# Stand-in matmuls at the start, and two VectorE pieces of step 12 placed sooner, in a spectral filter with a SiLU feed-forward block on one core

## The chip, the cores and the metric

One core of a Trainium2 chip runs the whole program. The metric is the device time in microseconds (us) of one execution; smaller is better. TensorE is called PE here, its weight loads PEld; VectorE is DVE, ScalarE is ACT, GpSimd is POOL, SyncE is SP.

## The reference

Eight sequences of 3008 tokens with 256 channels go through a global spectral filter, and the result of all tokens through a feed-forward block with SiLU:

```python
def _attn_ref(x, filt_r, filt_i) -> np.ndarray:
    X = np.fft.rfft(x, axis=1)
    F = (filt_r + 1j * filt_i)[None, :, :]
    Y = X * F
    y = np.fft.irfft(Y, n=x.shape[1], axis=1)
    return y.astype(np.float32)
...
def _moe_ref(x, w_in, w_out) -> np.ndarray:
    h = x @ w_in
    g = h * (1.0 / (1.0 + np.exp(-h)))
    return (g @ w_out).astype(np.float32)
```

w_in is 256 x 2048, w_out 2048 x 256, all in 32-bit floats.

## The kernel before, in words

**The filter.** Each batch's Fourier transform is split into short transforms (3008 = 47 x 64) that are matmuls with tables. Its stages have PSUM tiles by which the profile names them: pa (first stage, lines 401 and 425), pb (second stage, L542), a product with the filter on DVE (`multiply`, L635, which writes z and p) and two sums of products (`add`, L643 and L644), pc (the way back, L656 and L676), a store to DRAM and a load in another order, and pd (the last stage, L742), which is copied to y (L761).

**The feed-forward block.** Tokens are handled in 48 pairs of tiles of up to 256 columns each, and each pair in 8 steps, one for 256 of the 2048 hidden channels. The two 2 x 2 products of a step are formed with seven matmuls each in place of eight, from sums and differences. The operands' differences over tokens are made on DVE once per pair by `tokens(pair)`: three subtractions from y into a tile ty. `hidden(step)` makes the hidden values with matmuls into two PSUM banks, px and pyz (L1001), which ACT and DVE read: ACT copies partial sums to abc and takes SiLU (L1005), DVE adds (L972) to g. The half of pyz that a step calls zo is written by the matmul A12 and read by the first sum, g0; the half yo is written by S1 and S4 and read by the sums g2 and g1. `finish` makes the two last differences of g in the next step. `project(step)` multiplies g by w_out into four accumulator banks a0 to a3 (acc, L1093) one step later (LAG = 1), and `drain` copies a bank out, or adds it to what is there (s), when its pair has no matmul left on it. The first six steps are plain (`hidden_plain`, L1047), eight matmuls without the sums.

**What sets the order.** The schedule is written out by hand. The first batch's filter runs at the start, with nothing else for PE to do. From then on the loop goes over 384 steps of 8 rounds each. In a round the generators of `hidden` and `project` are advanced by one matmul each, and `until(time)` issues all pieces that are due in a list `pending`, sorted by time; `put(step, rnd, piece)` enters a piece. So the filter of the next batches is laid between the matmuls of the feed-forward block, piece by piece. A step in `opened` starts with the work of another stage, two projections of the step before ahead of it. Every engine runs its instructions in the order of issue.

The second batch (b = 1, at = 48) has a plan of its own in `plan`: for each of six groups g the pieces `forward`, `multiply` for two banks and `add` for two banks, with their steps and rounds counted from at. The forward of group 0 is issued when step 12 opens, so its listed place is not used. The pair 0 of tokens takes steps 0, 1 and 6 to 11, pair 1 steps 2 to 5 and 12 to 15, pair 2 steps 16 to 23. The accumulators of pair 0 are drained while step 12 runs.

**Banks at the start.** Until the loop starts, `bank` hands out the eight PSUM banks in turn by a counter `early[0]`: 2 banks f, then a0 to a3, then x and yz. The loop uses the banks by name.

**Stand-ins.** `idle(n, operand, m)` takes one bank and issues n matmuls of m columns by m columns whose result is never read:

```python
        ps = bank(0, "idle").rearrange("p a c -> p (a c)")
        rows = (wx_t if operand is None else operand)[:, 0:m]
        for _ in range(n):
            nc.tensor.matmul(out=ps[0:m, 0:m], lhsT=rows, rhs=rows, start=True, stop=True)
```

There are 26 of 36 columns ahead of pa, on a block of zeros, and 2 of 96 columns between the second batch's pa and the first batch's pd. Each matmul in 32-bit floats shows as two passes in the profile, a weight load and a matmul each.

Of the kernel before, what the change touches and what calls it, by code (L numbers as in the profile page):

```python
# [274 lines left out]
def kernel(  # L275
# [78 lines left out]
    def bank(b, name, spare=None):  # L354


        if early[0] is None and spare in ("x", "yz"):
            return xps.tile([128, 2, C], FP32, name=name, tag=spare)
        if early[0] is None and spare is not None:
            return accps.tile([128, 2, C], FP32, name=name, tag=f"a{spare}")  # L360
        if early[0] is None:
            return fps.tile([128, 2, C], FP32, name=name, tag="f")
        early[0] += 1
        k = early[0] % 8
        if k < 2:
            return fps.tile([128, 2, C], FP32, name=name, tag="f")
        if k > 5:
            return xps.tile([128, 2, C], FP32, name=name, tag="x" if k == 6 else "yz")
        return accps.tile([128, 2, C], FP32, name=name, tag=f"a{k - 2}")
# [451 lines left out]
    def put(step, rnd, piece, *args):  # L821

        pending.append((step + rnd / ROUNDS, len(pending), lambda: piece(*args)))
# [3 lines left out]
    def plan(b, part):  # L827

        at = STEPS * b

        if b > 1:
            put(at - {2: 80, 3: 120}.get(b, 128), 0, part["reverse_x"])
            early_fold = (-73, ((-68, 3), (-68, 5), (-65, 3), (-64, 3))), (-89, ((-82, 5), (-81, 3), (-81, 5), (-75, 5)))
            for f, step, load, places, ends in (
                    (0, -64, *early_fold[b > 2], ((1, 0), (1, 3))),
                    (1, -56, -63, ((-61, 5), (-60, 3), (-60, 5), (-59, 3)), ((1, 3), (2, 3))),
                    (2, -48, -55, ((-52, 3), (-52, 5), (-51, 5), (-50, 5)), ((1, 3), (2, 3)))):
                put(at + load, 4 if load == -89 else 0, part["load_fold"], f)
                for k, (fold_step, rnd) in enumerate(places):
                    put(at + fold_step, rnd, part["fold"], f, k)  # L840
                put(at + step, 7, part["stage1_fold"], f)
                put(at + step, 7, part["evict_fold"], f)
                for q, (after, rnd) in enumerate(ends):
                    put(at + step + after, rnd, part["pairs_fold"], f, q)
                joined.add(at + step)
                opened.add(at + step + 1)
            put(at - 47, 0, part["load_fold"], 3)
            for k, (step, rnd) in enumerate(((-45, 3), (-45, 5), (-44, 3), (-44, 5))):
                put(at + step, rnd, part["fold"], 3, k)
            early_out.add(at - 43)  # L850
            open_step(at - 43, (part["stage1_fold"], 3), (part["evict_fold"], 3))
            put(at - 43, 3, part["pairs_fold"], 3, 0)
            put(at - 43, 5, part["pairs_fold"], 3, 1)
            return plan_two(b, part)
        put(at - 38, 0, part["load_t2"], 0)
        put(at - 38, 0, part["load_t2"], 1)
        for g, places in enumerate((
                ((-36, 3), (-36, 5), (-35, 3), (-35, 5), (-34, 5)),
                ((-35, 6), (-34, 3), (-33, 3), (-33, 5), (-32, 1)),
                ((-32, 7), (-31, 0), (-31, 2), (-28, 5), (-27, 2)),  # L860
                ((-27, 3), (-27, 5), (-26, 5), (-25, 3), (-24, 3)),
                ((-24, 7), (-23, 0), (-23, 2), (-20, 2), (-20, 5)),
                ((-20, 3), (-19, 3), (-19, 5), (-18, 3), (-18, 5)))):
            pieces = (("forward", g), ("multiply", g, 0), ("multiply", g, 1), ("add", g, 0), ("add", g, 1))
            for (step, rnd), (piece, *args) in zip(places, pieces):
                if piece != "forward" or g in (1, 3, 5):
                    put(at + step, rnd, part[piece], *args)
        open_step(at - 36, *last_part[0](5), (part["forward"], 0))
        for g, step in ((0, -32), (2, -24), (4, -16)):
            put(at + step, 7, part["inverse"], g, 2)  # L870
            if g < 4:
                pending.append((at + step + 7 / ROUNDS, 10 ** 6 + 9, lambda g=g: part["forward"](g + 2, ACCS)))
                joined.add(at + step)
            put(at + step, 7, part["even"], g, 0, 2)
            put(at + step, 7, part["even"], g, 1, 2)
            put(at + step + 1, 5, part["rows"], g, 0, 2)
            put(at + step + 2, 3, part["rows"], g, 1, 2)
        plan_rest(b, part)
# [11 lines left out]
    def plan_two(b, part):  # L890

        at = STEPS * b
        put(at - 41, 3, part["load_t2"], 0)
        put(at - 41, 3, part["load_t2"], 1)
        for g, step, places in (
                (0, -40, ((-39, 3), (-38, 3), (-38, 5), (-36, 3), (-36, 5), (-35, 3))),
                (2, -32, ((-31, 0), (-31, 2), (-29, 5), (-28, 3), (-28, 5), (-27, 3))),
                (4, -24, ((-23, 0), (-23, 2), (-22, 3), (-21, 3), (-21, 5), (-19, 3)))):
            if g:
                plan_inverse(at + step, part, g - 2, *([((4, 3), (4, 5), (5, 5), (6, 3))] if g == 4 else []))  # L900
                opened.add(at + step + 1)
            put(at + step, 7, part["forward_two"], g)
            put(at + step, 7, part["free_two"], g)
            pieces = (("multiply_two", 0, 0), ("multiply_two", 0, 1), ("add_two", 0),
                      ("multiply_two", 1, 0), ("multiply_two", 1, 1), ("add_two", 1))
            for (place, rnd), (piece, *args) in zip(places, pieces):
                put(at + place, rnd, part[piece], g, *args)
        plan_inverse(at - 16, part, 4)
        plan_rest(b, part)

    def open_step(step, *pieces):

        opened.add(step)
        for piece, *args in pieces:
            pending.append((step - 0.06, len(pending), lambda piece=piece, args=args: piece(*args)))
# [62 lines left out]
    def tokens(pair):  # L978

        n, yt = pairs[pair][3], channels(pair)  # L980
        t = typool.tile([128, 4, CH], FP32, name=f"ty_{pair}", tag="ty")
        combine(v, t[:, 0:2, 0:n], yt[:, :, n:2 * n],
                yt[:, 0, 0:2 * n].rearrange("p (a n) -> p a n", a=2), ALU.subtract)
        combine(v, t[:, 2, 0:n], yt[:, 1, n:2 * n], t[:, 0, 0:n], ALU.subtract)
        combine(v, t[:, 3, 0:n], yt[:, 1, 0:n], t[:, 2, 0:n], ALU.subtract)
        ty[pair] = t
# [337 lines left out]
    def idle(n, operand=None, m=128):  # L1324
# [5 lines that stand above are left out]
# [8 lines left out]
    wide_rows = d_t[0:96].rearrange("p s r n -> p (s r n)")[:, 0:256]  # L1338
    blank = w_t.rearrange("p j c w n -> p (j c w n)")[0:96, 6144:6272]
    v.memset(blank, 0.0)  # L1340
    idle(26, operand=blank, m=36)

    part, second = spectral(0), spectral(1)
    part["load_first"]()
# [86 lines left out]
    def halves_of(*gs):  # L1431
        for g in gs:
            for i in range(2):
                part["store_half"](g, i, 1, gp)
    halves_of(2, 3)
    idle(2, m=96)
    early[0] -= 1
    part["stage3"](0)
    out_of(3, 3, copy=act)
# [23 lines left out]
    for b in range(1, B):  # L1463
        plan(b, second if b == 1 else spectral(b))
# [28 lines left out]
    per = len(PAIRS) * 2  # L1493


    combines = ((-2, 1), (6, 1), (11, 5), (22, 1), (26, 6), (38, 1))
    stores = (((10, 1), (10, 5)), ((19, 1), (23, 5)), ((31, 1), (31, 5)), ((35, 1), (35, 5)),
              ((43, 1), (43, 5)), ((50, 1), (51, 1)))
    for pair in range(len(pairs)):
        step, rnd = combines[pair % per] if pair > 2 else ((5, 2), (11, 1), (12, 1))[pair]  # L1500
        pending.append((pair // per * STEPS + step + rnd / ROUNDS, 98, lambda pair=pair: tokens(pair)))
        for chunk in range(2 if pair < len(pairs) - 1 else 0):
            step, rnd = stores[pair % per][chunk] if pair else (14, 1 + 4 * chunk)
            pending.append((pair // per * STEPS + step + rnd / ROUNDS, 99 + chunk,
                            lambda pair=pair, chunk=chunk: output(pair, chunk)))
# [65 lines left out]
```

## Time and profile before

| | |
|---|---|
| timed runs | 2484.73, 2486.55, 2486.83 us; median 2486.55 |
| profiled execution | 2485.27 us, its span 2483.1 us |
| busy in the span | PE 100%, PEld 86%, DVE 70%, ACT 44%, POOL 18% |
| PE by tile | acc 1513.1 us, px and pyz of L1001 1555 us (overlapping), all other lines 60 us or less |
| stand-ins | 52 passes of 36 columns, 4 passes of 96 columns |
| DMA | 69 GB/s mean over the span, 16 engines nearly full from 2 to 30 us |

Times in the profile count from the start of the span. A row of the timeline gives the start, the time taken, engine, line, operation, the tile written and those read, the shape, how many instructions were merged into it, and in brackets the idle time before it with what ended that. A row of waits reads: who waited, for whom, microseconds in total, how many times, the longest. Matmuls overlap in the pipe, so the duration of one says less than the distance from one start to the next.

### The profile page before, as it was taken

The numbers are of one execution on the slowest core, as the hardware profiler recorded it, in microseconds if no ns is written. First come the engines' busy times: TensorE is split into PE (matmuls) and PEld (weight loads), VectorE is DVE, ScalarE is ACT, GpSimd is POOL, SyncE is SP. The second block draws the span as 40 slices with busy tenths as digits, with TensorE's granted clock in tenths as the row PEclk, the third lists the DMA queues.
The fourth block names the chain that finished last, engine by engine and source line by source line (L and its number), as shares of the span: only waits on it lengthen the run. The fifth ranks groups of instructions, "written<-read, shape, count | busy, mean of one in ns | idle before, by whom it ended". The sixth has DMA issues, their size and how long they took to land.

```text
span 2483.1 us, 42315 instructions
## 1 busy us (share of the span) xinstructions
PE 2472.1 (100%) x16272; PEld 2124.9 (86%) x16272; DVE 1748.4 (70%) x3577; ACT 1087.1 (44%) x2986; POOL 438.9 (18%) x683
## 2 busy tenths in 40 slices
PE   9999999999999999999999999999999999999999
PEld 6888888888888888888888888889888888888988
DVE  7876777777777777786777767777777767655544
ACT  4534444444444444444444444444444444444443
POOL 4121112112221112211221112211221121101100
PEclk9999999999999999999999999999999999999999
DMA  8432225203242033320333114221142211200000
GB/s 327 148 98 77 74 63 117 63 14 93 61 109 61 25 78 81 96 54 26 88 83 89 49 29 108 60 69 43 51 98 47 56 51 32 59 22 9 17 10 17
DMA packets 139881, 170.68 MB, mean 69 GB/s; under 512 B 20972, under 2 KB 113484, under 8 KB 139148
## 3 DMA queue, kind: packets, MB, share of 16 engines
q1 hardware_dynamic: 116416, 121.74, 18.4%
q0 software_dynamic: 22272, 44.89, 6.9%
q8 instruction: 128, 2.10, 0.4%
q10 hardware_dynamic: 992, 1.36, 0.2%
q14 instruction: 73, 0.60, 0.1%
HBM read 96.06 MB, written 81.26 MB: 71 GB/s over the span
## 4 chain that ended last, share of the span: by engine, by line
PE 99%; DVE 0%; DMA 0%; POOL 0%; ACT 0%; issue 0%; SPq 0%; DVEq 0%
PE acc L1093 46%; PE px L1001 26%; PE pyz L1001 19%; PE pd L779 1%; PE pf L504 1%; PE pc L598 1%; PE pb L560 1%; PE pa L401 1%; PE pc L676 0%; PE px L1047 0%; PE pyz L1047 0%; PE pb L542 0%; PE pd L742 0%; PE pc L656 0%; DMA d<-w_t 0%; DMA w_t<-d 0%
## 5 line engine op out<-in xcount | busy, mean ns | idle before, releaser
L1093 PE MATMUL acc<-g,w_t 128*128 128x256 f32 (+1 forms) x5388 | 1513.1, 376 | 3.0 <-ACT o L792 2.5
L1093 PEld LDWEIGHTS acc<-g,w_t 128*128 128x128 f32 x5388 | 1019.8, 190 | 153.1 <-ACT o L792 15.3
L972 DVE TENSOR_TENSOR g<-pyz,abc 128x256 f32<-128x256 f32 (+1 forms) x1134 | 472.3, 416 | 468.2 <-ACT abc L1022 228.4
L972 DVE TENSOR_TENSOR g<-g 128x512 f32<-128x512 f32 (+1 forms) x1134 | 581.3, 513 | 193.8 <-ACT g L1005 180.8
L1001 PE MATMUL px<-ty,w_t 128*128 128x256 f32 (+1 forms) x2268 | 665.5, 375 | 0.0
L1005 ACT ACTIVATE g<-g 128x256 f32<-128x256 f32 (+1 forms) x1134 | 465.4, 410 | 231.9 <-DVE g L972 231.9
L972 POOL TENSOR_TENSOR s<-s 128x256 f32<-128x256 f32 (+1 forms) x331 | 254.3, 785 | 1436.4 <-DVE s L1121 981.8
L1001 PEld LDWEIGHTS px<-ty,w_t 128*128 128x128 f32 x2268 | 427.9, 190 | 52.1 <-issue 0.8
L1001 PE MATMUL pyz<-y,w_t 128*128 128x256 f32 (+1 forms) x1512 | 444.0, 375 | 1.1 <-DVE g L972 1.1
L1001 PEld LDWEIGHTS pyz<-y,w_t 128*128 128x128 f32 x1512 | 279.4, 189 | 42.3 <-DVE g L972 2.9
L1016 ACT COPY abc<-px 128x256 f32<-128x256 f32 (+1 forms) x378 | 139.1, 368 | 366.6 <-PE px L1001 366.6
L1005 ACT ACTIVATE g<-px 128x256 f32<-128x256 f32 (+1 forms) x378 | 143.5, 380 | 298.1 <-PE px L1001 298.0
L1022 ACT COPY abc<-px 128x256 f32<-128x256 f32 (+1 forms) x378 | 139.2, 368 | 307.3 <-PE px L1001 307.2
L1001 PE MATMUL px<-y,w_t 128*128 128x256 f32 (+1 forms) x756 | 223.5, 377 | 0.0
L1001 PE MATMUL pyz<-ty,w_t 128*128 128x256 f32 (+1 forms) x756 | 222.1, 376 | 0.0
L1001 PEld LDWEIGHTS px<-y,w_t 128*128 128x128 f32 x756 | 141.7, 189 | 21.1 <-DVE q L800 1.9
L1001 PEld LDWEIGHTS pyz<-ty,w_t 128*128 128x128 f32 x756 | 139.9, 190 | 20.2 <-DVE g L972 0.4
L1009 ACT COPY abc<-px 128x256 f32<-128x256 f32 (+1 forms) x378 | 133.0, 352 | 34.5 <-PE px L1001 34.5
L524 POOL DMA_DIRECT2D d<-tf x96 | 48.5, 505 | 212.9 <-DVE tf L454 212.9
L1121 ACT COPY s<-acc 128x512 f32<-128x512 f32 (+2 forms) x99 | 56.1, 566 | 49.0 <-issue 28.5
L619 POOL DMA_DIRECT2D d<-low x36 | 22.3, 618 | 292.5 <-DVE low L615 279.0
L494 DVE TENSOR_TENSOR uf<-x_all 120x512 f32<-120x512 f32 (+1 forms) x72 | 60.2, 864 | 0.3 <-issue 0.3
(134 smaller groups left out, 1390.2 us busy)
## 6 DMA issues: line engine op xcount, KB each, us to landing
t<-d SPq DMA_DIRECT2D x84, 256.0 KB
t<-d SPq DMA_DIRECT2D x224, 96.0 KB
out_dram<-s SPq DMA_DIRECT2D x64, 256.0 KB
d<-q POOLq DMA_DIRECT2D x48, 256.0 KB, 5.3
x_all<-in_x_dram SPq DMA_DIRECT2D x96, 96.0 KB
x_all<-xr SPq DMA_DIRECT2D x96, 96.0 KB
d<-tf POOLq DMA_DIRECT2D x96, 96.0 KB, 2.7
d<-tq POOLq DMA_DIRECT2D x96, 96.0 KB, 2.8
```

The source lines that it names most:

```text
L401: nc.tensor.matmul(out=ps[q], lhsT=wx3_t[rows, k], rhs=xs[j][rows, k], start=(k == 0), stop=(k == 2), skip_group_check=True)
L494: nc.vector.tensor_tensor(out=out, in0=in0, in1=in1, op=op)
L504: nc.tensor.matmul(out=ps[q][32 * k:32 * k + 32], lhsT=wq_t[rows, k], rhs=rhs[k][rows], start=True, stop=True)
L524: nc.gpsimd.dma_start(out=d1[par, :, grp, at:at + 4], in_=part[rows].rearrange("p q n c -> p (q n) c"))
L972: eng.tensor_tensor(out=out, in0=in0, in1=in1, op=op)
L1001: nc.tensor.matmul(out=out, lhsT=w_t[:, jp, c, 0], rhs=rhs, start=start, stop=True, skip_group_check=True)
L1005: nc.scalar.activation(out=g[:, k, 0:n], in_=g[:, k, 0:n] if src is None else src, func=AFT.Silu)
L1009: nc.scalar.copy(out=sums[:, 0, 0:n], in_=xo)
L1016: nc.scalar.copy(out=sums[:, 1, 0:n], in_=xo)
L1022: nc.scalar.copy(out=sums[:, 2, 0:n], in_=xo)
L1093: nc.tensor.matmul(out=acc[pair][i][:, h, 0:n], lhsT=w_t[:, jp, OUT_PLACE.get(c, c), 1], rhs=g[:, k, 0:n], start=i not in touched, stop=la ...
L1121: copy(out=dst, in_=src)
```

## The change

The stand-ins ahead of pa become 64 of 15 columns. The two between pa and pd go, and with them their step of the bank counter, so that stage pd of groups 0 to 2 takes other banks. The first filter product of the second batch, group 0 and bank 0, moves from step 12 round 5 to step 12 round 3. The tokens' sums of pair 2 move from step 12 round 1 to round 0.

```diff
         for g, places in enumerate((
-                ((-36, 3), (-36, 5), (-35, 3), (-35, 5), (-34, 5)),
+                ((-36, 3), (-36, 3), (-35, 3), (-35, 5), (-34, 5)),
                 ((-35, 6), (-34, 3), (-33, 3), (-33, 5), (-32, 1)),
...
     v.memset(blank, 0.0)
-    idle(26, operand=blank, m=36)
+    idle(64, operand=blank, m=15)
...
     halves_of(2, 3)
-    idle(2, m=96)
     early[0] -= 1
     part["stage3"](0)
     out_of(3, 3, copy=act)
...
     for pair in range(len(pairs)):
-        step, rnd = combines[pair % per] if pair > 2 else ((5, 2), (11, 1), (12, 1))[pair]
+        step, rnd = combines[pair % per] if pair > 2 else ((5, 2), (11, 1), (12, 0))[pair]
```

In DVE's order of instructions the three subtractions come to stand ahead of the sum g0 of step 12 instead of behind `finish`, and the two products ahead of the sum g2 of step 12 instead of between the drains of banks 2 and 3. On ACT, POOL and SP the order stays as it was.

## The prediction

> **What bounds the kernel now.** I read the page's totals and its chain first, then who waited for whom on PE, then the timeline around each edit.
>
> ```profile
> PE 2472.1 (100%) x16272; PEld 2124.9 (86%) x16272; DVE 1748.4 (70%) x3577; ACT 1087.1 (44%) x2986; POOL 438.9 (18%) x683
> PE 99%; DVE 0%; DMA 0%; POOL 0%; ACT 0%; issue 0%; SPq 0%; DVEq 0%
> ```
>
> PE is busy for 2472.1 of 2483.1 us and carries 99% of the chain that ends last. So an edit counts only where PE stands still or works for nobody. The view of PE's waits has six rows; the edits touch two of them and the stand-ins ahead of pa:
>
> ```profile
> PE pd L742 <- DMA w_t<-d: 1.4, 2, 0.9
> PE pyz L1001 <- DVE g L972: 1.1, 1, 1.1
> ```
>
> The first wait is for a transfer between pa and pd. The second is one stop of 1.1 us on VectorE (DVE).
>
> **Step 12: the tokens' sums and the filter product.** Both are DVE work of step 12 (48 - 36), and the instruction order of the changed kernel differs on DVE only there. The timeline before:
>
> ```profile
> 134.80 0.42 DVE L972 TENSOR_TENSOR g<-pyz,abc 128x256 f32<-128x256 f32 x1 [1.59 <-ACT abc L1009]
> ...
> 135.94 0.65 DVE L972 TENSOR_TENSOR ty<-y 128x480 f32<-128x480 f32 x1
> ...
> 136.62 0.85 DVE L972 TENSOR_TENSOR ty<-y,ty 128x240 f32<-128x240 f32 x2
> ...
> 137.39 0.42 DVE L972 TENSOR_TENSOR g<-pyz,abc 128x256 f32<-128x256 f32 x1
> 137.73 0.42 DVE L972 TENSOR_TENSOR s<-acc,s 128x256 f32<-128x256 f32 x1
> ...
> 139.05 0.68 DVE L635 TENSOR_TENSOR z<-pb,filt 128x512 f32<-128x512 f32 x1
> ...
> 139.28 0.67 PE L1093 MATMUL acc<-g,w_t 128*128 128x256 f32 x2
> 139.65 0.68 DVE L635 TENSOR_TENSOR p<-pb,filt 128x512 f32<-128x512 f32 x1
> 140.25 0.42 DVE L972 TENSOR_TENSOR s<-acc,s 128x256 f32<-128x256 f32 x1
> 140.58 0.42 DVE L972 TENSOR_TENSOR g<-pyz,abc 128x256 f32<-128x256 f32 x1
> ...
> 141.05 0.70 PE L1001 MATMUL pyz<-y,w_t 128*128 128x256 f32 x2 [1.10 <-DVE g L972]
> ```
>
> From 134.80 on DVE never rests. Its last piece, the sum g1 out of yo's half of the pyz bank (140.58, over at 141.00), frees that bank, and A12 of step 13 waits for it until 141.05. Yet DVE had stood idle for 1.59 us before 134.80.
>
> The tokens' three subtractions take the time from 135.94 to 137.39, 1.46 us. One round sooner they follow the y copy that ends at 133.21, so by the same pitch they are over near 134.67, still ahead of the ACT copy that the sum at 134.80 needs (over at 134.73). That sum isn't late. The ty buffer that they write was last read at about 129.8, by A22 of step 11. In the place they leave, the two products fit: 135.94 and 136.54 by their pitch of 0.60, over at 137.22. Both read pb, whose matmuls ended at 133.63. The sum g2 stays at 137.39, because it waits for an ACT copy that ends at 137.32. The four drains of banks 1 and 2 stay too, the last from 138.72 to 139.14, with their accumulator waits unchanged. Then the drain of bank 3 follows at 139.05 instead of 140.25. Its last matmul is not the row at 139.28 (that is the first projection of step 12) but the one before S4, which ends at 138.58, so nothing holds it. g1 runs from 139.38 to 139.80, and A12 starts at 139.85. The projection ahead of it streams until 139.79 (two passes of 0.215), so 0.06 us of the stop is left: **141.05 - 139.85 = 1.20 us less**. The bounds are 1.10, the idle time in the row of waits, and 1.26, the whole distance to 139.79.
>
> What is late next: the z and p products of the other bank, 143.83 to 145.11 before, have to be over before the next pb matmuls take the f banks (146.00). All of it moves forward together; only POOL's eight adds (138.30 to about 145.3) don't. Beside them the two late subtractions took 1.49 us (142.42) instead of 0.88. If that happens again, 0.6 us of the 0.9 us between 145.11 and 146.00 go, and PE still doesn't wait. Neither piece issues a DMA, and the orders of SP, POOL and ACT are the same as before.
>
> **The stand-ins at the start.** 52 passes (two for each matmul) become 128.
>
> ```profile
> 1.08 3.34 PE L1329 MATMUL idle<-w_t 96*36 96x36 f32 x52 [1.08 <-DVE w_t L1340]
> ...
> 4.35 0.52 PEld L401 LDWEIGHTS pa<-w_t,wx 32*128 32x128 f32 x8
> ...
> 5.37 0.35 PEld L401 LDWEIGHTS pa<-w_t,wx 32*128 32x128 f32 x4 [0.50 <-DMA w_t<-in_x_first_dram]
> 6.22 0.35 PEld L401 LDWEIGHTS pa<-w_t,wx 32*128 32x128 f32 x4 [0.50 <-issue]
> ...
> 9.18 10.24 DVE L405 STREAM_TRANSPOSE w_t<-pa 128x512 f32<-128x512 f32 x16 [8.15 <-PE pa L401]
> 9.42 0.19 PEld L401 LDWEIGHTS pa<-w_t,wx 32*128 32x128 f32 x4 [0.23 <-issue]
> 9.85 0.19 PEld L401 LDWEIGHTS pa<-w_t,wx 32*128 32x128 f32 x4 [0.23 <-issue]
> ```
>
> The stand-ins follow each other every 60.1 ns and the last one has streamed at 4.22. That is 1.67 ns for each of 36 columns. The same pace is in the pa rows: one set of 512 columns every 0.85 us at first (5.37, 6.22), and every 0.43 us from about 8.3 on (9.42, 9.85). So TensorE runs at half its clock until then; the trace's own record of the granted clock starts at 8.32.
>
> 15 columns at 1.67 ns are 25.0 ns, and 128 passes 3.20 us: 1.10 + 3.20 = 4.30. pa starts at 4.35 because its table, the last of 16 parts, lands at 4.17. So by streaming alone the new stand-ins stay hidden, with 0.05 us to spare. What no row shows is whether a pass of 15 columns keeps to 25 ns. The lower end is 25.0 ns. The upper end is 60.1 ns, as if narrower passes were no shorter: 7.7 us, so pa 4.4 us later. Between them, pd's 190 passes of 47 columns take 3.09 us, 16.3 ns each at full clock but on alternating quarters of the array; doubled for the half clock that is 32.6 ns (4.17 us, pa 0.9 us late). I take 25 to 28 ns, nearest to the 36-column row, since this is the same instruction on the same rows and shows no fixed part; a 256-column pass at full clock takes 215.6 ns where its columns account for 213.3, so a fixed part of some 2 to 3 ns is the most I grant. 28 ns cost 0.3 us; I put down **0.1 us more**.
>
> The Trainium skill ("TensorE: Matmul & The Clock Gate", Back-to-back issue gap) gives narrow matmuls a floor of about 60 cycles, 25 ns at the full clock. Read as cycles at the half clock that is 50 ns: pa 3.1 us late, and by the sum below 2487.8 us; no row here shows such a floor.
>
> The products of 15 x 15 instead of 36 x 36 are work for nobody, on zeros. Code is fetched 152 instructions sooner; PE's first 16 KB fetch, at 14.28 before, comes near 4.3 among the input loads, and takes 1.1 us with another 256 instructions to go. I cost it at nothing.
>
> **The two stand-ins between pa and pd.**
>
> ```profile
> 47.68 0.58 PE L1329 MATMUL idle<-wx_t 96*96 96x96 f32 x4
> ...
> 48.82 0.29 PE L742 MATMUL pd<-wi_t,w_t 64*64 64x47 f32 x2 [0.56 <-DMA w_t<-d]
> ...
> 49.99 3.09 PE L742 MATMUL pd<-wi_t,w_t 64*64 64x47 f32 x190 [0.89 <-DMA w_t<-d]
> ```
>
> They end at 48.26. pd's first pair waits for a transfer until 48.82, the rest until 49.99 for the one that lands at 49.86, and that transfer hangs on a store issued at 40.22. So 0.58 us of PE work goes and nothing starts sooner: **0**. The line also moves the bank counter by one. pd of group 0 goes to an f bank and a0, group 1 to a3 and x, group 2 to a1 and a2. The latest of these to come free is the f bank, copied by ACT from 47.78 to 48.36, under the transfer. px of step 0 (53.01) then waits for the DVE copy of group 1 instead of ACT's; they end at 52.75 and 52.63, both in time.
>
> What is lost is cover: PE has almost no work from 47.75 to 49.99, 2.24 us, where its longest stop after 8.3 was about 1.1. The Trainium skill (same page, "HAM oscillation") says that the clock falls back after a gap over some 3.4 us. By that rule nothing falls here and the second rival has no chance; the trace, whose longest gap is half of this one, can't bear it out, so the rival keeps a small one.
>
> **Sum.** -1.20 + 0.10 + 0 = -1.10 us. The profiled execution took 2485.27 us, so its successor would take 2484.2. But the three timed runs are 2484.73, 2486.55 and 2486.83, median 2486.55, 1.3 above it. I see a cause at the start: a set of pa costs 0.43 us more whenever the clock opens a set later, and that moment need not be the same in each execution. The middle of all four is 2485.9, and I work from there: **2484.8**. A measurement of this kernel tells apart about 0.2%, 5 us; almost everything below lies within that.
>
> **Rivals.**
>
> - *The stand-ins outlast the table* (slower than before). Place: PE, before pa. For it: no row of so narrow a pass on one part of the array, and a margin of 0.05 us. Against: 60.1 ns is streaming to the last digit. Price: 128 x (p - 25.4 ns). It decides from p = 34.8 ns, where it eats the 1.2 us. At 32.6 ns it gives 2485.6; at the upper end, 60.1 ns, 2489.1, above the 2485.9 I start from. Chance 0.13, of it 0.05 beyond 34.8 ns. The skill's floor, cited above, belongs here.
> - *The clock falls between pa and pd.* For it: 2.24 us with next to nothing. Against: gaps of 1.02 and 1.10 didn't do it. Price by the start: it took from 4.35 to 8.32, 3.97 us of dense work, to open, at half pace 2.0 us lost: 2486.8. Chance 0.07.
> - *The stand-ins open the clock sooner.* For it: more and denser instructions. Against: 3.2 us of 36 columns didn't. Price: pa's third piece lands only at 6.84 and its second quarter at 8.70, so the second batch of transposes starts at 11.5 instead of 11.74: 0.24 us, 2484.5. Chance 0.10.
> - *The DVE reordering changes nothing*, because POOL's adds or a late product keep g1 where it is: 2486.0. The order speaks against it, and no step above rests on a margin under 0.1 us except the tokens'. Chance 0.08.
>
> The forecast has 0.62. **Range**: low end, the lowest execution 2484.73 less 1.44 (1.20 and 0.24) less 0.5 of spread, 2482.8; high end, the highest 2486.83 less 1.2 plus 1.7 for most of the first two rivals, 2487.3. Faster by over 0.2% 0.02, slower by over 0.2% 0.03 (two of the prices together, on a high execution), within it 0.95.
>
> **What would show it.** Right: no PE wait on DVE g at A12 of step 13, the drain of bank 3 at once behind that of bank 2, g1 0.4 us after S4's end (139.01) and no longer 1.6; stand-ins that end by 4.35; pd's long row still released by the transfer and 3.1 us long. Wrong: pa's first set after 4.5, a pd row longer than 3.3 us, px rows at double pace after it, or the zo sum of step 12 later than 1.3 us after A11's start (1.24 before).

## The result, and the profile after

The changed kernel takes **2489.91 us** in the median (2486.52 to 2492.3, 19 runs), the kernel before 2485.12 (2484.39 to 2487.56, 19 runs) beside it: a ratio of 1.0017, 95% interval [1.001, 1.0025]. It is slower by some 4.8 us by the medians and 4.2 us by the ratio, where the forecast was 1.1 us faster. The profiled execution took 2491.88 us with a span of 2489.8, 6.7 more than the span before; it lies 2.0 above the median.

The page's totals and the shares of its chain, as they were shown of before:

```profile
PE 2475.2 (99%) x16344; PEld 2124.1 (85%) x16344; DVE 1749.7 (70%) x3577; ACT 1088.5 (44%) x2986; POOL 439.3 (18%) x683
PE 98%; DMA 1%; issue 0%; POOL 0%; ACT 0%; DVE 0%; SPq 0%; DVEq 0%; POOLq 0%
```

PE is busy 3.1 us longer and idle 3.6 us longer. The view of PE's waits says where the idle time is:

```profile
PE pd L742 <- issue: 4.2, 1, 4.2
...
PE pd L742 <- DMA d<-w_t: 0.9, 1, 0.9
PE pd L742 <- DMA w_t<-d: 0.7, 1, 0.7
```

The row `PE pyz L1001 <- DVE g L972: 1.1` is gone, as forecast. In its place stands one stop of 4.2 us in pd, for "issue": nothing that the profile shows was being waited for. The timeline of PE around it:

```profile
50.86 2.39 PE L742 MATMUL pd<-wi_t,w_t 64*64 64x47 f32 x145 [0.94 <-DMA d<-w_t]
57.42 1.52 PE L742 MATMUL pd<-wi_t,w_t 64*64 64x47 f32 x45 [4.18 <-issue]
58.87 2.07 PE L1047 MATMUL px<-y,w_t 128*128 128x256 f32 x4
60.74 1.91 PE L1047 MATMUL pyz<-y,w_t 128*128 128x256 f32 x4
62.45 1.26 PE L1047 MATMUL px<-y,w_t 128*128 128x256 f32 x4
```

The first of these px rows before:

```profile
53.01 1.13 PE L1047 MATMUL px<-y,w_t 128*128 128x256 f32 x4
```

The 190 passes of pd that were one row of 3.09 us are cut in two. The first 145 run at 16.3 ns each, then PE stands still from 53.24 to 57.42, and the last 45 take 1.52 us, 33.8 ns each: double pace. px goes on so (2.07 for four passes, 1.13 before) until about 62.9. The trace's record of the granted clock agrees: half speed from 56.08 to 62.90, which is in no view of before.

The span adds up, by the starts of rows in the two timelines: pd's long row starts 0.87 later (50.86 and 49.99), the stop takes 4.18, and the half clock 2.8 (0.8 in the last 45 passes of pd, 2.0 in px and pyz). That is 7.85. At px of step 12 the delay is still 7.85 (141.41 and 133.56), and behind step 12 it is 6.7: the DVE moves gave back 1.2.

**What the stop is.** Among the page's DMA queues is one for code:

```profile
q8 instruction: 128, 2.10, 0.4%
```

128 packets, 2.10 MB, hence 16 KB each. PE's instructions come in such blocks: PE has 32,896 records (matmuls, weight loads and the semaphore waits of its sequencer), 257 to a packet, and 255.7 to 257.6 in all thirteen kernels. I took the start and end of each block from the trace's DMA records, and numbered PE's records in order of their starts. The sixth block decides:

| | record 1473 issued | sixth block fetched | record 1729 issued | record 1730 |
|---|---|---|---|---|
| before | 51.30 | 54.94 to 55.90 | 58.30 | 58.51 |
| after | 51.10 | 55.11 to 56.04 | 53.05 | 57.42 |

In both, the block arrives near 56. Before, PE needs it at 58.51, 2.6 us after the landing. After, PE has issued everything it holds at 53.05, because 144 instructions more stand ahead of it (152 in the stand-ins at the start, less 8 between pa and pd), so that the end of the block falls into pd, where 256 instructions last 2.1 us instead of up to 28 us (at 0.215 us for a pair of weight load and matmul). It goes on 1.38 us after the landing; by that lag the kernel before had some 1.2 us to spare. **So far this is a theory; the experiments test it.**

### The profile page after: what moved, and what is told of

Its sections match the earlier page's. It is cut to its first block, busy times and chain, and to the rows that moved or that the text cites. A ratio compares the mean times of both kernels' runs of the same rounds, so it can differ in the third digit from the quotient of the medians.

```text
span 2489.8 us, 42457 instructions
## 1 busy us (share of the span) xinstructions
PE 2475.2 (99%) x16344; PEld 2124.1 (85%) x16344; DVE 1749.7 (70%) x3577; ACT 1088.5 (44%) x2986; POOL 439.3 (18%) x683
## 4 chain that ended last, share of the span: by engine, by line
PE 98%; DMA 1%; issue 0%; POOL 0%; ACT 0%; DVE 0%; SPq 0%; DVEq 0%; POOLq 0%
PE acc L1093 46%; PE px L1001 26%; PE pyz L1001 19%; PE pd L779 1%; PE pf L504 1%; PE pc L598 1%; PE pb L560 1%; DMA e_t<-e_tbl 1%; PE pc L676 0%; PE px L1047 0%; PE pyz L1047 0%; PE pd L742 0%; PE pb L542 0%; PE pa L425 0%; PE pc L656 0%; DMA w_t<-in_x_first_dram 0%
## 5 line engine op out<-in xcount | busy, mean ns | idle before, releaser
L972 DVE TENSOR_TENSOR g<-pyz,abc 128x256 f32<-128x256 f32 (+1 forms) x1134 | 472.4, 417 | 465.8 <-ACT abc L1022 228.3
L972 DVE TENSOR_TENSOR g<-g 128x512 f32<-128x512 f32 (+1 forms) x1134 | 582.1, 513 | 193.8 <-ACT g L1005 180.9
L1001 PE MATMUL px<-ty,w_t 128*128 128x256 f32 (+1 forms) x2268 | 664.8, 375 | 0.0
L972 POOL TENSOR_TENSOR s<-s 128x256 f32<-128x256 f32 (+1 forms) x331 | 254.1, 785 | 1442.1 <-DVE s L1121 982.0
L1001 PEld LDWEIGHTS px<-ty,w_t 128*128 128x128 f32 x2268 | 427.5, 190 | 52.6 <-issue 0.8
L1001 PE MATMUL pyz<-y,w_t 128*128 128x256 f32 (+1 forms) x1512 | 443.6, 375 | 0.0
L1001 PEld LDWEIGHTS pyz<-y,w_t 128*128 128x128 f32 x1512 | 279.1, 189 | 41.4 <-DVE g L972 1.8
L1001 PE MATMUL px<-y,w_t 128*128 128x256 f32 (+1 forms) x756 | 223.2, 377 | 0.0
L1001 PE MATMUL pyz<-ty,w_t 128*128 128x256 f32 (+1 forms) x756 | 221.9, 375 | 0.0
L1001 PEld LDWEIGHTS px<-y,w_t 128*128 128x128 f32 x756 | 141.6, 189 | 21.2 <-DVE q L800 1.9
L1001 PEld LDWEIGHTS pyz<-ty,w_t 128*128 128x128 f32 x756 | 139.8, 190 | 20.5 <-DVE g L972 0.6
```

What stands on the lines that cost most here:

```text
L972: eng.tensor_tensor(out=out, in0=in0, in1=in1, op=op)
L1001: nc.tensor.matmul(out=out, lhsT=w_t[:, jp, c, 0], rhs=rhs, start=start, stop=True, skip_group_check=True)
```

## The experiments

Each expectation is the text on record ahead of the run. "Stop" is the wait on "issue" in the view of PE's waits, in pd where no other tile is named; the shift counts PE's matmuls and weight loads ahead of pd against the kernel before. Ratios are to the kernel before, timed beside it on the same chip.

| run | shift | stop, us | half clock after the opening | median, us | before | ratio [95%] |
|---|---|---|---|---|---|---|
| changed kernel | +144 | 4.18 | 56.08 to 62.90 | 2489.91 | 2485.12 | 1.0017 [1.001, 1.0025] |
| DVE moves only | 0 | none | none | 2486.01 | 2486.45 | 0.9997 [0.9988, 1.0006] |
| 64 of 15 only | +152 | 4.78 | 55.16 to 61.99 | 2491.43 | 2486.45 | 1.0017 [1.0008, 1.0026] |
| none between pa and pd | -8 | none | none | 2487.05 | 2486.45 | 1.0002 [0.9993, 1.0011] |
| all but the 64 of 15 | -8 | none | 51.56 to 54.98 | 2486.13 | 2486.45 | 0.9998 [0.999, 1.0007] |
| changed, 84 of 15 | +224 | none in pd, 1.0 in pc | 53.13 to 56.54 | 2486.37 | 2487.15 | 0.9999 [0.999, 1.0008] |
| changed, 44 of 15 | +64 | 2.76 | 51.00 to 54.41, 57.83 to 61.24 | 2489.83 | 2487.15 | 1.0012 [1.0003, 1.0021] |
| 38 of 15 in the gap | +144 | 4.29 | 56.95 to 63.78 | 2491.57 | 2487.15 | 1.0018 [1.0009, 1.0026] |
| changed, two loads later | +144 | 1.70 | 65.22 to 72.05 | 2494.47 | 2487.15 | 1.0035 [1.0021, 1.0048] |
| changed, one load later | +144 | 2.42 | 101.09 to 104.50 | 2488.7 | 2487.14 | 1.0009 [1.0, 1.0018] |
| DVE moves, 13 of 72 | -52 | none in pd, 0.4 in pc | none | 2485.27 | 2487.14 | 0.9996 [0.9987, 1.0005] |
| DVE moves, 84 of 15 | +232 | none in pd, 1.0 in pc | none | 2486.12 | 2487.14 | 0.9997 [0.9988, 1.0006] |

**The change in its parts.** First the DVE moves alone:

```diff
-                ((-36, 3), (-36, 5), (-35, 3), (-35, 5), (-34, 5)),
+                ((-36, 3), (-36, 3), (-35, 3), (-35, 5), (-34, 5)),
-        step, rnd = combines[pair % per] if pair > 2 else ((5, 2), (11, 1), (12, 1))[pair]
+        step, rnd = combines[pair % per] if pair > 2 else ((5, 2), (11, 1), (12, 0))[pair]
```

> Before with the two VectorE moves alone. All theories: PE's wait for g1 at the opening of step 13 goes, 1.1 to 1.2 us less than before (about 2484.0 against 2485.1). If the moves themselves cost something, the time is not below before.

2486.01 against 2486.45, no stop, and no wait of PE on DVE g. By the medians 0.4 us went and not the 1.1 to 1.2 expected; 1.2 us can't be told from nothing in these times, and only the trace shows them. Then the stand-ins at the start alone:

```diff
-    idle(26, operand=blank, m=36)
+    idle(64, operand=blank, m=15)
```

> Before with 64 stand-ins of 15 columns alone; the two between pa and pd stay. Code theory: 152 instructions more ahead of pd shift the ends of PE's 256-instruction code blocks into pd, whose instructions are used up faster than the next block comes: a stop of about 4 us inside pd that waits for nothing the profile shows, a half clock behind it, 4 to 7 us slower than before. Rival (the cover between pa and pd was what counted): no stop, within 0.5 us of before. Rival (only the start is late): pa 0.3 us late and no more than 1 us slower.

The whole loss is here, with the two stand-ins in the gap still in place:

```profile
49.89 2.36 PE L742 MATMUL pd<-wi_t,w_t 64*64 64x47 f32 x140 [0.71 <-DMA w_t<-d]
57.03 1.62 PE L742 MATMUL pd<-wi_t,w_t 64*64 64x47 f32 x50 [4.78 <-issue]
```

Five passes of pd fewer than in the changed kernel come ahead of the stop, since the 8 instructions of the gap, worth four passes with their loads, count ahead of it again. By number it is the same place, behind record 1729. Third, the two stand-ins of the gap alone:

```diff
-    idle(2, m=96)
```

> Before without the two stand-ins between pa and pd (and with the shift of banks that goes with them). Code theory: 8 instructions fewer, the ends of the blocks stay where they were, no stop: within 0.5 us of before. Rival (cover): the clock falls during or behind pd, 2 us or more slower than before. Rival (other banks): a new wait of pd or px for a copy.

1.0002 [0.9993, 1.0011]: no loss that can be told. Last, both DVE moves and the empty gap, with the old stand-ins at the start (against the changed kernel):

```diff
-    idle(64, operand=blank, m=15)
+    idle(26, operand=blank, m=36)
```

> The changed kernel with the 26 stand-ins of 36 columns put back. Code theory: 1.2 us less than before, about 2484.0, and some 6 us less than the changed kernel, no stop in pd. Rival (cover): still slower than before by 2 us or more.

No stop, 2486.13, which is 2 us above what I gave. Its profiled execution shows something else, half clock from 51.56 to 54.98, in most of pd:

```profile
50.70 4.58 PE L742 MATMUL pd<-wi_t,w_t 64*64 64x47 f32 x190 [1.05 <-DMA d<-w_t]
```

The 190 passes took 3.09 us before and without the two stand-ins of the gap. That is the second rival of the prediction, taken up below.

**More stand-ins, and fewer.** If the number of stand-ins or a late start were the cause, 84 would cost more than 64, and 44, which end well ahead of the table, nothing. If the place of the block's end is the cause, it is the other way round. The edits to the changed kernel:

```diff
-    idle(64, operand=blank, m=15)
+    idle(84, operand=blank, m=15)
```

> The changed kernel with 84 stand-ins of 15 columns in place of 64. Theory (place of the code blocks): PE's instructions ahead of pd shift by 224 against the kernel before instead of 144, so the block of 256 that runs out inside pd is asked for near 45.5 us, before the DMA engines fill at 47, and the next one runs out only behind pd. No stop on 'issue' in pd. Price of the extra stand-ins: 40 passes x 27.3 ns = 1.1 us, pa from about 5.7. The sum: 4.2 us of stop less and 2.8 us of half clock less than the changed kernel, 1.1 more at the start: about 6 us faster than the changed kernel's profile, 2486 to 2488 us in all, unless the clock falls in the gap between pa and pd (then 2488 to 2490). Rival 1 (more stand-ins or a later start are what costs): slower than the changed kernel, 2491 to 2493. Rival 2 (the missing cover between pa and pd stops PE): as the changed kernel plus 1.1, with the stop of 4 us still in pd.

With 84 there is no stop in pd, and the time is that of the kernel before (0.9999), though pa starts at 5.67, 1.3 us later than before. The sixth block is fetched from 46.93, ahead of the three weight loads that SP issues from 48.29 on. The engines were not free then (a DMA share of 0.94 from 46 to 47), so full engines alone don't make a block late. The clock fell in pd, behind the gap, in the profiled execution, and its 2488.28 is within what that case was given; the median, 2486.37, lies in the range given without it.

PE does stop elsewhere in this run:

```profile
PE pc L676 <- issue: 1.0, 1, 1.0
```

It stops behind record 1217, two times 256 ahead of 1729: the fourth block landed at 35.92, and the next matmul started at 37.41, 1.49 us on. The run with 84 and the cover, below, stops at the same record, and the one with 13 of 72 behind record 961, another 256 ahead. These shorter stops were not expected, and they bear the theory out at two more blocks.

```diff
-    idle(64, operand=blank, m=15)
+    idle(44, operand=blank, m=15)
```

> The changed kernel with 44 stand-ins of 15 columns, which end near 3.5 us, well ahead of the table. Theory (place of the code blocks): a shift of 64 instructions still puts the end of the block into the last tenth of pd (near 52.8 us instead of 53.2) and the request near 50.8, inside the time of full DMA engines: the stop stays, 3 to 4.5 us long, and the clock falls after it or not by its phase; 2489 to 2492 us. Rival 1 (stand-ins that last too long, pa late): pa at 4.35 again and no loss left, about 2485 to 2486. Rival 2 (cover): the clock's fall of up to 2 us, no stop on 'issue', about 2487.

```profile
50.42 4.48 PE L742 MATMUL pd<-wi_t,w_t 64*64 64x47 f32 x185 [0.81 <-DMA w_t<-d]
57.66 0.36 PE L742 MATMUL pd<-wi_t,w_t 64*64 64x47 f32 x5 [2.76 <-issue]
```

The stop is there with 20 stand-ins fewer than in the changed kernel, five passes from the end of pd. Its size is below what I gave (2.76, not 3 to 4.5). The row says why: the 185 passes took 4.48 us, at half clock since 51.00, so PE ran out only at 54.70; the block landed at 56.23, as late as ever.

**The same shift with the start left alone.** This run has the DVE moves, the start of before, and 38 stand-ins in the gap, which covers it better than before. Against the kernel before, beside the DVE moves:

```diff
-    idle(2, m=96)
+    idle(38, m=15)
```

> The kernel before with both VectorE moves, its 26 stand-ins of 36 columns at the start kept, and 38 of 15 columns between pa and pd in place of 2 of 96. Start as before, the gap covered better than before (76 passes, about 1.0 us at full clock), and the instructions ahead of pd shifted by 144, as in the changed kernel. Theory (place of the code blocks): pd stops on 'issue' for 4 to 5 us though start and cover are fine; with the half clock after it 2490 to 2493 us. Rivals (the start; the missing cover): no stop, 2485 to 2486.5.

```profile
48.13 2.06 PE L1329 MATMUL idle<-wx_t 96*15 96x15 f32 x76
50.25 2.80 PE L742 MATMUL pd<-wi_t,w_t 64*64 64x47 f32 x146
57.34 1.52 PE L742 MATMUL pd<-wi_t,w_t 64*64 64x47 f32 x46 [4.29 <-issue]
```

Nothing idle ahead of pd, the stop all the same, and 1.0018. Start and cover are ruled out as causes of the stop. (The 76 passes took 2.06 us, by their records one every 25 ns, not the 1.0 I had worked out from streaming at full clock.)

**Why the block is late.** SP issues three raw weight loads of 512 KB each just ahead of pd. Here, in the changed kernel, two of them go behind the stores that follow:

```diff
-    weights(3, 4, 5)
+    weights(3)
...
-    weights(6)
+    weights(6, 4, 5)
```

> The changed kernel with the raw weight loads of steps 4 and 5 (512 KB each) issued behind the stores that follow them on SP, so that the DMA engines have less queued when PE asks for its code near 51.1 us. Theory (a code fetch queued behind full DMA engines): the block lands sooner, and the stop shrinks from 4.2 us to 0 to 2.5; 2486 to 2490 us by what is left of the stop and the half clock. Rival (a code fetch takes 4 to 5 us from its request whatever the DMA engines do, or PE stops for something else): the stop stays at 4.2 us and the time at 2490 to 2492.

Its waits on PE:

```profile
PE px L1047 <- DVE w_t L1256: 5.9, 1, 5.9
...
PE pd L742 <- issue: 1.7, 1, 1.7
```

The stop shrank as expected; the total did not, since the weights of step 4 now come too late and PE waits 5.9 us for them. That cost I had not foreseen. So another run moves only one load:

```diff
-    weights(3, 4, 5)
+    weights(3, 4)
...
-    weights(6)
+    weights(6, 5)
```

> The changed kernel with only the raw weight load of step 5 (512 KB) issued behind the stores, that of step 4 left where it was: half of what e8 took out of the queues ahead of the code block. Theory (the code block waits behind what the DMA engines have queued): 512 KB at the pace of these loads, some 180 GB/s, are 2.9 us; the stop of 4.2 us goes to 1 to 2.5 us, and the wait for step 4's weights that cost e8 5.9 us is gone or below 1 us: 2486.5 to 2489.5 us. Rival (the code block waits for something else in e8's order): the stop stays at 4 us, 2490 to 2492.

The stop is 2.42 and the time 2488.7, both as expected, though another 2.2 us go at 100.20: the conversion of step 5's weights, now later on DVE, stands ahead of a sum of g that PE waits for. The fetches side by side, from the DMA records:

| | loads ahead | record 1473 | fetch starts | lands | PE goes on |
|---|---|---|---|---|---|
| changed kernel | 3 | 51.10 | 55.11 | 56.04 | 57.42 |
| 38 of 15 in the gap | 3 | 50.90 | 54.90 | 55.84 | 57.34 |
| changed, one load later | 2 | 50.45 | 52.02 | 53.69 | 55.01 |
| changed, two loads later | 1 | 50.26 | 51.65 | 52.54 | 54.10 |

The fetch itself takes 0.9 us, in one row 1.7; what varies is when it starts, and that follows the loads: the SP queue (q1) holds the 16 engines at 0.94 to 1.03 from 50 to 55 in the changed kernel and at under 0.8 from 50 on with two loads moved. POOL's queue (q0) gets its first packets through within 1.2 us of the code in all four. The second load moved brought only 0.37 us more, so it isn't simply 2.9 us a load, and how the engines choose between the queues stays open.

**The cover by itself, and the smaller number.** The run with 84, with the two stand-ins of the gap put back; against the kernel before, beside the DVE moves:

```diff
-    idle(26, operand=blank, m=36)
+    idle(84, operand=blank, m=15)
```

> The kernel before with both VectorE moves and 84 stand-ins of 15 columns, the two between pa and pd kept: the run with 84 of 15 again, with the cover back. Theory (blocks and cover are two separate causes): no stop in pd, as there; and no fall of the clock behind the gap, which took 1.5 to 2 us there. 1.1 us later at the start, 1.2 less at step 12: 2484.5 to 2486.5 us, the same as before and up to 1.5 us below the run without cover. Rival (two stand-ins of 96 columns, 0.6 us, are too little to hold the clock): the clock falls for 3.41 us in pd again and the time is that of the run without cover.

```profile
51.94 3.09 PE L742 MATMUL pd<-wi_t,w_t 64*64 64x47 f32 x190 [0.22 <-DMA raw<-in_moe_w_dram]
```

3.09 us at full clock and no stop in pd, where the run without them has 4.58 us, partly at half clock. The medians, 2486.12 and 2486.37, don't tell the two apart. Last, half as many instructions for as many columns, beside the DVE moves:

```diff
-    idle(26, operand=blank, m=36)
+    idle(13, operand=blank, m=72)
```

> The kernel before with both VectorE moves and 13 stand-ins of 72 columns in place of 26 of 36: as many columns at the start, half the instructions, the two stand-ins between pa and pd kept. Theory (place of the code blocks): the shift is -52 instructions, so the sixth block runs out 52 instructions later than before, in px (near 61 us), and its code lands near 56: no stop, more room than before. The start as before (26 passes of 120 ns end near 4.2), the clock doesn't fall. The 1.2 us of the VectorE moves are left: 2484 to 2486.5 us, ratio 0.9990 to 1.0000, as far as 1.2 us can be told at all. Rival (number of columns and not of instructions opens the clock or holds it, or wide stand-ins outlast the table): the time of the kernel before plus 0 to 2 us.

2485.27 against 2487.14, the lowest ratio of all, 0.9996 [0.9987, 1.0005], with one execution at 2491.61 that I can't explain. No kernel here beats the one before by more than the measurement leaves open.

## Why the prediction was wrong

**The step that failed** is the end of the part on the stand-ins: "Code is fetched 152 instructions sooner; PE's first 16 KB fetch, at 14.28 before, comes near 4.3 among the input loads, and takes 1.1 us with another 256 instructions to go. I cost it at nothing." I looked at the first block only (it was fetched at 7.01 and hurt nobody), and priced it by its duration, 1.1 us. Every later block moved too. The question for each was when it can start among the transfers, and how long 256 instructions last at that place: the sixth waits 4.0 us before 0.93 us of fetching, while the 256 instructions in stock last 2.1 us. The stop measured 4.18 us, and 4.78 with the 64 alone, with 2.8 us of half clock behind it. Both lay open in the trace of before: the DMA share is 0.93 to 1.03 there from 51 to 55 (the last figure but one of each row of this view of before), and the instructions can be counted.

```profile
51.00:53.00 2.00, 2.00 (x137) 1.96 (x129) 1.35 (x3) 1.44 (x3) 2.00 (x5) 1.00 0.93 307
53.00:55.00 2.00, 2.00 (x14) 1.79 (x10) 1.90 (x5) 0.86 (x2) 2.00 (x4) 1.00 1.03 404
```

Three of the four signs of being wrong came: pa's first set at 4.61, after 4.5; pd's long row, 3.9 us without the stop, over 3.3; and px at double pace.

The Trainium skill ("Runtime: NRT & Kernel Launch", Instruction fetch mechanics) says the same of the blocks, 256 instructions fetched through a queue of the engine's own while the current ones execute, and calls the cost of crossing "mostly hidden". By that rule the sum would have stayed at -1.1 us. The traces agree on the blocks and not on the cost: it was hidden in the kernel before, and six kernels stopped for 1.7 to 4.8 us behind record 1729, three others for 0.4 to 1.0 us at an earlier block.

**The rival that came closest** was the clock between pa and pd, at 0.07 with 2.0 us. In the changed kernel the clock fell, but behind the stop and not in the gap, and 2.8 us went. In three kernels without cover it fell just behind the gap, in pd, and in "all but the 64 of 15" pd then took 1.5 us longer, where 2.0 was priced. So the rival was real, and the reason for its small chance was wrong: I took the Trainium skill's rule ("TensorE: Matmul & The Clock Gate", HAM oscillation) that only a gap over some 3.4 us does it. What the records show is a window of 3.413 us that runs on from the moment the clock opened. Every fall comes a whole number of windows after it: 14 in the changed kernel (8.29 + 14 x 3.413 = 56.07), 12 or 13 in the three without cover. The fall goes with how little PE did in that window. Two windows, of "all but the 64 of 15" and of the changed kernel; the columns are the window, its length, then busy time and instructions of PE, PEld, DVE, ACT and POOL, granted clock, DMA share, GB/s:

```profile
48.15:51.56 3.41, 1.15 (x59) 1.09 (x62) 0.76 (x2) 0.46 (x1) 1.08 (x3) 1.00 1.01 289
```

```profile
49.25:52.66 3.41, 2.12 (x123) 2.03 (x123) 0.73 (x2) 0.91 (x3) 1.46 (x3) 1.00 0.95 297
52.66:56.07 3.41, 0.58 (x40) 0.52 (x33) 1.84 (x3) 0.83 (x2) 3.21 (x7) 1.00 1.01 398
```

The clock fell at the end of the first (1.15 us of PE work) and of the third (0.58), and not at the end of the second (2.12), which holds the gap of the changed kernel. The Trainium skill ("TensorE: Matmul & The Clock Gate", What's actually happening) does call the window free-running, where it tells of warming up. The length of the gap doesn't decide: with 44 of 15 a gap of 1.8 us between pa and pd's long row was followed by a fall, and with none between pa and pd one of 2.0 us was not. Where the gap lies in the windows differs, since the clock opens between 5.75 and 10.04 us in these runs. Busy time doesn't sort the windows cleanly either (last section).

**What held.** The stand-ins: 25 to 28 ns a pass forecast, 26.8 measured from start to start, and pa starts at 4.61 instead of 4.35.

```profile
1.08 3.60 PE L1329 MATMUL idle<-w_t 96*15 96x15 f32 x128 [1.08 <-DVE w_t L1340]
4.61 5.78 PE L401 MATMUL pa<-w_t,wx 32*128 32x512 f32 x32
```

(The last pass starts at 4.49; the row's 3.60 holds the pipe's end too.) That ruled out the first rival, and the Trainium skill's floor read as 50 ns. Only the number is shown, not my reason for it: in the gap, at full clock, such a pass took 25 ns too, so more than the columns at the granted clock may set it. The 0.26 us are within the 0.3 that I had named, above the 0.1 that I put down. The other 0.6 by which pd is late doesn't belong to the stand-ins: the run with them alone starts pd's long row at 49.89, ahead of the kernel before (49.99). The row waits for a transfer; the DVE moves alone start it at 50.44 and the run with none between pa and pd at 50.56, and why the transfer lands when it does isn't shown.

Step 12, with DVE's order as derived; px of A11 starts at 141.41, 7.85 later than before:

```profile
143.78 0.68 DVE L635 TENSOR_TENSOR z<-pb,filt 128x512 f32<-128x512 f32 x1
144.38 0.68 DVE L635 TENSOR_TENSOR p<-pb,filt 128x512 f32<-128x512 f32 x1
145.19 0.42 DVE L972 TENSOR_TENSOR g<-pyz,abc 128x256 f32<-128x256 f32 x1
...
147.19 0.41 DVE L972 TENSOR_TENSOR g<-pyz,abc 128x256 f32<-128x256 f32 x1
```

Less 7.85 that is 135.93, 136.53, 137.34 and 139.34; forecast were 135.94, 136.54, 137.39 and 139.38. A12 starts at 147.66, less 7.85 at 139.81 (forecast 139.85). The gain of 1.2 us is shown in the trace; the rival that the order changes nothing is out.

**The range** held only what the listed mechanisms could do, and none of them was this one. 2489.91 is 2.6 us above its end. The loss lies just under the 0.2%, 5 us, from which the prediction counted slower, and it is clear of the noise all the same: the interval, 1.001 to 1.0025, leaves out 1.

**Open.** The profiled execution of the changed kernel lost more than its median (2491.88 and 2489.91); whether the others had a shorter stop or less half clock, no trace shows. That a block is asked for some 256 instructions ahead is read from fetches that start early (the sixth block with 1464 and 1466 records issued in the runs with 84, and the tenth, with the engines idle, with 2472 to 2558 issued, around 1729 + 768 = 2497); the request itself isn't in the trace. Why the sixth block got through full engines at 46.9 in the two runs with 84 and not from 51 on in the others isn't shown.

## What to carry to other kernels

Before an edit adds or removes instructions on an engine, count them against that engine's blocks of code: find the stages where a block is used up fastest and the DMA engines are fullest, and see whether a block's end is moved into one. A stop "on issue" in the middle of a uniform row, with nothing of the program to wait for, is the mark of it; the code queue's records and a count of instructions settle it. If it can't be avoided by order, the number of filler instructions is a free parameter: 13 wide ones or 84 narrow ones did no harm that the times can tell, though a block's end still stopped PE for 0.4 to 1.0 us, where 44 and 64 did.

## What the runs showed of the hardware

- PE's code block needs 1.32 to 1.56 us from landing to the next matmul in the six kernels that stopped in pd, and 1.41 to 1.49 us in the three that stopped in pc, beside 0.9 to 1.7 us of fetching and up to 4.6 us of waiting to start (up to 6.4 in pc).
- The stop is behind record 1729 in all six, with 44 or 64 stand-ins at the start or 38 in the gap: it belongs to the count of instructions and to no line. In three other kernels PE stopped behind record 1217 or 961, two or three times 256 earlier.
- The clock's falls and rises lie on multiples of 3.413 us from its first opening, in all kernels that show one (12, 13, 14, 15, 17 and 27 windows). It fell behind windows with 0 to 1.9 us of PE work and stayed with 1.7 to 2.7; ends on PE are modelled, and the threshold isn't closer than that.
- A stand-in of 15 columns came every 26 or 27 ns at the start, at half clock, and every 25 ns in the gap, at full clock: so short a pass isn't bound by its columns at full clock. The Trainium skill ("TensorE: Matmul & The Clock Gate", Back-to-back issue gap) has a floor of about 25 ns for narrow matmuls; taken as a time, and not as cycles of the granted clock, it lies near both.
